# Squares of the first seven-product phase kept on chip, its loads asked for earlier, and two weight sums moved ahead

## The chip, the cores and the metric

The kernel runs on one core of one Trainium2 chip. The metric is the device time of one execution in microseconds (us). TensorE does the matrix products (PE in the rows; PEld is its weight load), VectorE (DVE) and ScalarE (ACT) move results out of PSUM and do the elementwise work, GpSimd (POOL) scales operands in SBUF, and SyncE (SP) issues nearly all DMAs from one in-order queue.

## The reference, cut to what matters

```
# attention with decay, in blocks of 64 tokens (B=4, H=8, S=768, D=64)
intra = ((q_b @ k_b.T) * Dmask) @ v_b
inter = (q_b * lam_pow) @ kv_state
out_b = intra + inter
kv_state = lam_block * kv_state + (k_b * rev_pow).T @ v_b
# feed-forward on x = attention output, 3072 tokens x 512
h = x @ w_in          # 512 -> 2048
g = relu(h) ** 2
y = g @ w_out         # 2048 -> 512
```

## The kernel before

The 3072 tokens are 24 tiles of 128, or six groups of four tiles (512 tokens). Every float32 operand of the feed-forward part is split into a high and a low part (`wh` and `wl` hold those of weights and tokens), and a product is made of three matmuls: high by high, low by high, high by low.

Groups 0 and 1 are done plainly, 16 steps `f` each: `hidden` (12 matmuls, one 128-column piece of h), `square`, then `project` of the step before (12 matmuls into four `acc` banks). I call the 16 steps of group 1 "steps 0 to 15". In even steps `go(t, t + 1)` does the attention of tile t and begins that of the tile after it; in between the weights of the later phases are prepared: `weigh(n)` forms sums of w_in and writes them to DRAM (`ws`), and `fold(n)` forms sums of w_out (VectorE: `fold_whole` and `fold_sums`; then a ScalarE cast `fold_hi` and a VectorE subtraction `fold_lo`, which issues two DMAs to DRAM, `wt`). The dictionary `todo` says in which step a cast and its subtraction stand.

Groups 2 and 3 are then done together, as a 2 by 2 block product with seven products in place of eight. This is the first seven-product phase: eight blocks `quad(n)`, n = 0 to 7, each with `product(n, 0)` to `product(n, 6)` of six matmuls each, and between products 2 and 3 the attention `go(t)` of tile t = 16 + n. The weights of a product come from DRAM through the tile `ring`, asked for eight products ahead, by `stream(k + 8)` at the end of each product. A block gives four 128-column results: two sums `gs`, which live in four tiles `GT` and are squared in place one block later (`square_pair`), and two (`pa` and `pb`, in PSUM) that `square_in` squares into `E[2n]` and `E[2n + 1]`. The order of the work on each engine is the order in which the code stands.

Before the change, `E[0]` to `E[11]` are slices of `GT[2]` and `GT[3]`. These are needed for `gs` from block 4 on, so squares 0 to 7 are copied to DRAM (`es`, blocks 0 to 3) and read back in block 7 (`move` with a source), and squares 8 to 11 are copied on chip into free columns of `w_out` (`spare`). The loads of k, q, v of tile t + 2 (`load_qk`, `load_kv`) stand at the end of a block, behind `state`, and GpSimd's scaling of k (`scale_k`) behind them. `fold(0)` to `fold(5)` are done in blocks 1 to 6, and `fold(7)`, `fold(6)` in steps 0 and 1.

Then `gather_all(2)` multiplies by w_out, again with seven products, in 16 passes q of about 5 us: eight for one half of the result (squares `E`) and eight for the other (`GT`). Pass q reads the sums of one `fold`, which `fold_in` asks for two passes ahead, and the operands that `operands`, `operands_hi`, `operands_lo` prepare three passes ahead. `SEQ` is the order of the folds in the first eight passes: 4, 5, 6, 0, 7, 1, 2, 3. `between(q)` stands behind pass q: it reads the attention outputs (`ks`, eight DMAs) into `GT[0]` and `GT[1]`, forms their sums, and `rows_of` writes the operands of the second seven-product phase (`quad_all`, groups 4 and 5).

In `go`, ScalarE reads one element of the first attention bank into `mark`; TensorE's next writes to that bank wait for this read.

```
        product(n, 2, pd, True, False)
        go(t, None if last else t + 1, True)
        product(n, 3, pb, False, False)
        add(gs[1], pb, p1)
        product(n, 4, pa, False, True)
        square_in(f, pa)
        product(n, 5, pb, False, True)
        product(n, 6, pd, False, True)
        add(pb, pb, p1)
        add(gs[0], pd, gs[0])
        square_in(f + 1, pb)
```

Of the kernel before, what the change touches and what calls it, by code (L numbers as in the profile page):

```python
# [7 lines left out]
F32 = mybir.dt.float32  # L8
# [27 lines left out]
def body(ctx: ExitStack, tc: tile.TileContext, qT, kT, kvq, lam, w, out):  # L36
# [60 lines left out]
    def w_out(f):  # L97
        return NF + (f + 1) % NF
# [316 lines left out]

    def masked_by_half(t):
        a = wk.tile([P, 2, NPR, D], F32, name="a")
# [18 lines left out]

    def go(t, after, own=False):
        po, pn = (ps_acc, "acc") if own else (ps_a, "att")
        qo, qn = (ps_acc, "acc") if own else (ps_h, "h")
        o = [po.tile([P, DM], F32, name=pn) for _ in range(2)]  # L440
# [135 lines left out]
    def f32(x):  # L576
        return x.bitcast(F32)
# [141 lines left out]
    def fold_lo(n):  # L719
        x, (hi, lo) = FOLD.pop(n)  # L720
        sub(lo, x.rearrange("p a b -> p (a b)"), f32(hi))
        for i, y in enumerate((hi, lo)):
            nc.sync.dma_start(out=wt[n, :, :, i], in_=f32(y).rearrange("p (a b) -> p a b", a=4))

    E, OPS, TR = {}, {}, [None, None]
    GT = []
    es = dram.tile([NF // 2, P, DM], F32, name="es")
    ks = dram.tile([2 * G, P, DM], F32, name="ks")
    squares, spill = [], []

# [3 lines left out]
    def first_places():  # L734
        for tag in ("xh", "xl"):
            GT.append(wk.tile([P, 4, N], F32, name="gs", tag=tag))
        for tag in ("xh", "xl"):
            GT.append(wk.tile([P, 4, N], F32, name="gs", tag=tag))
        for f in range(3 * NF // 4):
            E[f] = GT[3 if f > 3 else 2][:, f % 4]  # L740

    def spare(i):
        j = w_out(4 * i)
        return [f32(x[:, j : j + 3 : 2, 2 * P :]) for x in (wh, wl)]

    def move(n, x, source=None):
        for j in range(2):
            f = 2 * n + j
            nc.sync.dma_start(out=x[j], in_=by_half(E[f] if source is None else source[f]))
            E[f] = x[j]  # L750

# [4 lines left out]
    def square_pair(n):  # L756
        x = GT[n // 2][:, 2 * n % 4 : 2 * n % 4 + 2].rearrange("p a b -> p (a b)")
        nc.scalar.activation(x, x, AF.Relu)
        nc.scalar.activation(x, x, AF.Square)

    def quad(n, prev):
        f, t = 2 * n, 4 * G + n
        last = n == NF // 2 - 1
        if n == 0:
            first_places()
        gs = [GT[n // 2][:, f % 4 + j] for j in range(2)]
        pa, pb = (ps_h.tile([P, N], F32, name="h") for _ in range(2))
        pd = ps_a.tile([P, N], F32, name="att")
        p1 = wk.tile([P, N], F32, name="p1", tag="gh")
        KEPT[t] = wk.tile([P, DM], F32, name="kept", tag="gl")  # L770
        product(n, 0, pa, True, False)
        nc.scalar.copy(p1, pa)
        if n:
            square_pair(n - 1)
        product(n, 1, pb, True, False)
        add(gs[0], pb, p1)
        if n > 1:
            fold_lo(n - 2)
        if n in (5, 6):
            move(n - 1, spare(3 * (6 - n)))  # L780
        if last:
            move(0, spare(1), es)
            move(1, spare(2), es)
            x = io.tile([P, 2 * DM], F32, name="qk_sb")
            move(2, [by_half(x[:, j * DM : (j + 1) * DM]) for j in range(2)], es)
            operands(1)
        if n == 0:
            project(*prev)
        product(n, 2, pd, True, False)
        if last:  # L790
            open_folds(0)
        go(t, None if last else t + 1, True)
        if not last:
            scale_q(t + 1)
        product(n, 3, pb, False, False)
# [8 lines left out]
        if n == NF // 2 - 2:  # L804
            for j in range(2):
                E[f + j] = mask.rearrange("p j a c -> p j (a c)")[:, j]
        if last:
            for j in range(2):
                E[f + j] = wk.tile([P, N], F32, name="kept", tag="a")
        square_in(f, pa)  # L810
        if 0 < n < NF // 2 - 1:
            fold(n - 1)
        product(n, 5, pb, False, True)
        if last:
            operands_hi(2)
        product(n, 6, pd, False, True)
        if last:
            open_folds(1)
            add(gs[0], pd, gs[0])
            operands_lo(1)  # L820
            operands(3)
            operands_hi(3)
            add(pb, pb, p1)
        else:
            add(pb, pb, p1)
            add(gs[0], pd, gs[0])
        square_in(f + 1, pb)
        if last:
# [4 lines left out]
        else:  # L833
            if n:
                fold_hi(n - 1)
            state(t, False)
            state(t + 1, True)
            if t + 2 < NT:
                load_qk(t + 2)
                load_kv(t + 2)  # L840
                scale_k(t + 2)
        nc.sync.dma_start(out=ks[n], in_=kept(t))
        if n < NF // 4:
            for j in range(2):
                nc.sync.dma_start(out=es[f + j], in_=E[f + j])
        if last:
            move(3, [by_half(x.rearrange("p a c -> p (a c)")) for x in (qpow, kv)], es)
        if n == NF // 2 - 2:
            operands(0)
# [25 lines left out]

    def quad_all(n):
        f = 2 * n
# [12 lines left out]
        add(u2, pb, p1)  # L890
        places_for(f)
        if last:
            operands(1)
# [36 lines left out]

    NQ = NF // 2
    SEQ = [4, 5, 6, 0, 7, 1, 2, 3] + list(range(NQ))
    MAP = [2, 0, 3, 1]
# [6 lines left out]
    def fold_in(q, j):  # L940
        if q < 2 * NQ:
            nc.sync.dma_start(
                out=f32(TR[q % 2][:, j]), in_=wt[SEQ[q], :, (1, 0, 2, 3)[j]].rearrange("p a b -> p (a b)")
            )

    def operands(q):
        par, n = q // NQ, SEQ[q]
# [37 lines left out]
    def gather(q, i, bank):  # L985
        k, n = q % NQ, SEQ[q]
        f = 2 * n
# [77 lines left out]
    def between(q):  # L1065
        two = [slice(0, 2), slice(2, 4)]
        flat = [[x[:, h].rearrange("p a d -> p (a d)") for h in two] for x in GT]
        (e0, e1), (d0, d1), (n0, n1), (f0, f1) = flat
        if q in (6, 8):
            j = (q - 6) // 2  # L1070
            for i in range(G):
                nc.sync.dma_start(
                    out=GT[j][:, :, i * C : (i + 1) * C], in_=ks[2 * i + j].rearrange("p (a b) -> p a b", a=KT)
                )
        if q == 10:
            sub(n0, d0, e0)
            sub(n1, d1, n0)
        if q == 12:
            sub(f0, d1, d0)
            sub(f1, e1, e0)  # L1080
            sub(f1, f1, f0)
            rows_of(8, GT[2][:, two[1]])
        if q == 13:
            rows_of(0, GT[0][:, two[0]])
# [195 lines left out]
    for f in range(NF):  # L1280
# [23 lines left out]
        if f % 2 == 0:  # L1304
# [5 lines left out]
            load_kv(t + 2)  # L1310
        if f < 2:
            fold(NF // 2 - 1 - f)
        if f in WEIGH:
# [16 lines left out]
    gather_all(2, between)  # L1330
    SEQ[:NQ] = range(NQ)
    MAP[:] = [3, 0, 2, 1]
    ORDER[:] = [0, 4, 6, 5, 1, 3, 2]
    for n in range(NF // 2):
        quad_all(n)
    gather_all(4, lambda q: None)
# [54 lines left out]
```

## Time and profile before

| | |
|---|---|
| time, median of 3 runs | 628.91 us (627.04, 628.91, 637.31) |
| the profiled execution: time / span | 625.99 us / 624.3 us |
| PE busy, DVE busy, ACT busy (share of the span) | 93%, 71%, 48% |
| chain that ended last: PE, DMA, DVE, issue | 55%, 14%, 13%, 7% |
| bytes moved by DMA | 145.58 MB, mean 233 GB/s |

A time in a row is counted from the start of the span. In brackets behind an instruction stands how long its engine had been idle and what ended that. "Clock" is the TensorE clock that the chip granted; 1.00 is 2.4 GHz, 0.5 is 1.2 GHz.

### The profile page before, as it was taken

Reading aid. Unit: us, or ns where it says so; the run is one execution under the profiler, and the core shown is the slowest. Engines: PE = TensorE matmul, PEld = TensorE weight load, DVE = VectorE, ACT = ScalarE, POOL = GpSimd, SP = SyncE. Lnnn points to the kernel's source line nnn. Section 1 sums busy time; section 2 is a strip of 40 time slices with the busy share of each in tenths; the row PEclk is TensorE's granted clock in tenths of the full one; section 3 lists DMA queues with packets and bytes.
Section 4 is the critical chain, followed back from the end, with each engine's and each line's share of the span. In section 5 each row is a group of like instructions: output and inputs, shape, how many; then the busy total and the mean of one; then the engine's idle time right before and its main releaser. Section 6 shows DMA issues by size and latency. Waiting matters only on the chain.

```text
span 624.3 us, 13452 instructions
## 1 busy us (share of the span) xinstructions
PE 580.3 (93%) x5308; PEld 501.4 (80%) x5308; DVE 442.2 (71%) x734; ACT 297.5 (48%) x522; POOL 96.0 (15%) x106
## 2 busy tenths in 40 slices
PE   9998999998999998788888879998969999999997
PEld 7886888887887886666666669997958888899997
DVE  6899999748887767355555699579564455997942
ACT  4678787544455553444444484343223233652420
POOL 5321213314322223102122100000000000000000
PEclk9999999999999999999979989999989999999999
DMA  8847656235998874769879887698666777676863
GB/s 307 334 141 250 220 201 207 97 135 180 305 362 295 279 234 139 246 204 307 287 248 321 264 307 240 212 303 273 186 203 183 221 194 201 205 227 205 278 205 122
DMA packets 88909, 145.58 MB, mean 233 GB/s; under 512 B 7952, under 2 KB 40720, under 8 KB 88848
## 3 DMA queue, kind: packets, MB, share of 16 engines
q1 hardware_dynamic: 84208, 139.49, 69.4%
q10 hardware_dynamic: 4640, 5.24, 2.3%
q8 instruction: 42, 0.69, 0.5%
q14 instruction: 19, 0.16, 0.1%
HBM read 109.05 MB, written 33.55 MB: 228 GB/s over the span
## 4 chain that ended last, share of the span: by engine, by line
PE 55%; DMA 14%; DVE 13%; issue 7%; SPq 3%; ACT 3%; POOL 2%; ACTq 0%; DVEq 0%; POOLq 0%
PE h L674 13%; PE acc L998 13%; PE h L514 6%; PE att L998 6%; DMA kv_sb<-in_kvq 6%; PE att L674 4%; PE h L998 3%; DMA folds<-wt 3%; DVE sums L214 2%; DMA ws<-parts 2%; PE acc L544 2%; PE acc L549 2%; PE acc L545 2%; DVE rec L214 2%; POOL kv_sb L395 1%
## 5 line engine op out<-in xcount | busy, mean ns | idle before, releaser
L674 PE MATMUL h<-wh,ring 128*128 128x512 f32 x320 | 92.1, 411 | 8.6 <-DVE kv_sb L214 5.3
L674 PEld LDWEIGHTS h<-wh,ring 128*128 128x128 f32 x320 | 62.0, 198 | 24.9 <-DVE kv_sb L214 6.1
L998 PE MATMUL acc<-folds,wh 128*128 128x256 f32 x384 | 71.6, 286 | 6.7 <-DMA folds<-wt 6.7
L998 PEld LDWEIGHTS acc<-folds,wh 128*128 128x128 f32 x384 | 60.7, 194 | 7.0 <-issue 7.0
L970 ACT CAST wh<-sums 128x1024 fp32r<-128x1024 f32 x32 | 33.6, 1050 | 52.8 <-DVE sums L214 16.7
L998 PE MATMUL acc<-folds,wl 128*128 128x256 f32 x192 | 54.9, 286 | 0.0
L214 DVE TENSOR_TENSOR wl<-sums,wh 128x1024 fp32r<-128x1024 f32 x38 | 46.3, 1219 | 8.3 <-ACT wh L970 8.3
L674 PE MATMUL h<-wl,ring 128*128 128x512 f32 x160 | 51.7, 405 | 0.0
L544 PE MATMUL acc<-wh,gh 128*128 128x512 f32 x128 | 50.3, 393 | 0.0
L549 PE MATMUL acc<-wh,gl 128*128 128x512 f32 x128 | 49.9, 390 | 0.0
L545 PE MATMUL acc<-wl,gh 128*128 128x512 f32 x128 | 49.9, 390 | 0.0
L503 POOL TENSOR_TENSOR kvd<-kv,qpow 128x256 f32<-128x256 f32 x27 | 21.8, 807 | 123.0 <-DVE kv L214 101.3
L521 ACT ACTIVATE h<-h 128x512 f32<-128x512 f32 x32 | 18.7, 584 | 45.0 <-PE h L514 44.8
L529 DVE TENSOR_TENSOR gl<-h,gh 128x512 fp32r<-128x512 f32 x32 | 21.9, 684 | 23.6 <-ACT h L524 23.6
L998 PEld LDWEIGHTS acc<-folds,wl 128*128 128x128 f32 x192 | 37.4, 195 | 0.0
L674 PEld LDWEIGHTS h<-wl,ring 128*128 128x128 f32 x160 | 31.5, 197 | 7.3 <-issue 0.3
L214 DVE TENSOR_TENSOR gs<-h,p 128x512 f32<-128x512 f32 x16 | 11.1, 691 | 36.4 <-PE h L674 35.8
L514 PE MATMUL h<-xh,wh 128*128 128x512 f32 x128 | 36.0, 403 | 0.8 <-DVE a L214 0.2
L514 PE MATMUL h<-xh,wl 128*128 128x512 f32 x128 | 34.5, 391 | 1.6 <-DVE wl L159 1.6
L674 PE MATMUL att<-wh,ring 128*128 128x512 f32 x128 | 34.4, 390 | 0.0
L514 PE MATMUL h<-xl,wh 128*128 128x512 f32 x128 | 34.3, 389 | 0.0
L214 DVE TENSOR_TENSOR wl<-gs,wh 128x256 fp32r<-128x256 f32 (+2 forms) x39 | 25.8, 672 | 11.2 <-ACT wh L1062 9.6
(252 smaller groups left out, 1425.0 us busy)
## 6 DMA issues: line engine op xcount, KB each, us to landing
folds<-wt SPq DMA_DIRECT2D x128, 256.0 KB, 3.9
ring<-ws SPq DMA_DIRECT2D x112, 256.0 KB, 3.1
raw<-in_w SPq DMA_DIRECT2D x30, 512.0 KB, 4.3
kv_sb<-in_kvq SPq DMA_DIRECT2D x22, 512.0 KB, 5.8
ws<-parts SPq DMA_DIRECT2D x32, 256.0 KB, 4.4
qk_sb<-in_kT SPq DMA_DIRECT2D x22, 256.0 KB, 4.3
qk_sb<-in_qT SPq DMA_DIRECT2D x22, 256.0 KB, 4.7
out_x<-qk_sb ACTq DMA_DIRECT2D x16, 256.0 KB, 6.4
```

What stands on the lines that cost most here:

```text
L214: lambda o, x, y, op=op: V.tensor_tensor(out=o, in0=x, in1=y, op=op)
L395: nc.gpsimd.tensor_tensor(out=x, in0=x, in1=y.broadcast_to([P, NPR, 2, D]), op=ALU.mult)
L503: nc.gpsimd.tensor_tensor(out=kvd, in0=d, in1=qpow[:, :, D - 1 : D].broadcast_to([P, NPR, D]), op=ALU.mult)
L514: nc.tensor.matmul(h, wt[:, f, kt * P : (kt + 1) * P], x[:, kt], start=k == 0, stop=k == 11)
L521: nc.scalar.activation(h, h, AF.Relu)
L529: V.tensor_tensor(out=gl, in0=r, in1=gh.bitcast(F32), op=ALU.subtract)
L544: nc.tensor.matmul(accs[m][i], gh[:, cs], wh[:, j], start=f == 0, stop=False)
L545: nc.tensor.matmul(accs[m][i], gh[:, cs], wl[:, j], start=False, stop=False)
L549: nc.tensor.matmul(accs[m][i], gl[:, cs], wh[:, j], start=False, stop=end)
L674: nc.tensor.matmul(bank, x[:, part_, kt], t[:, q + kt], start=start and z == 0, stop=stop and z == 5, skip_group_check=True,)
L970: nc.scalar.copy(o_, x)
L998: nc.tensor.matmul(bank[:, r * 2 * P : (r + 1) * 2 * P], x, y, start=k == 0 and r == 0 and z == 0, stop=k == NQ - 1 and z == 2, skip_group ...
```

## The change

- Loads: `load_qk(t + 2)` and `load_kv(t + 2)` stand directly behind `go(t)` in the middle of the block. `scale_k(t + 2)` stays at the end.
- Squares: the DRAM tile `es` is gone (8 DMAs out, 8 back, of 256 KB each). `E` gets 16 homes on chip; nine squares are copied on chip at the ends of blocks 1, 2, 4, 5, 6 (`MOVES`). In return `p1`, `kept` and the attention tile `a` have one buffer each in the phase, not two.
- Sums of w_out: `fold(7)` before step 0, `fold(6)`, `fold(5)`, `fold(4)` in steps 0, 1, 8; `fold(0)` to `fold(3)` in blocks 1 to 4, spread over two blocks each.
- Order: `add(pb, pb, p1)`, the second `square_in` and both `state` stand ahead of product 6; in block 0 `project` stands ahead of products 0 and 1.
- Passes: the folds are read in their natural order; the DMAs of `between` stand behind passes 9 and 11 (were 6 and 8), its sums and `rows_of` one or two passes later, and `rows_of(6)`, `rows_of(4)` stand in the first block of `quad_all` (`late`).

```diff
-    def go(t, after, own=False):
+    def go(t, after, own=None):
...
-            masked_by_half(after)
+            masked_by_half(after, own)
...
+        only.extend(wk.tile([P, N], F32, name=n, tag=t) for n, t in (("p1", "gh"), ("kept", "gl"), ("a", "a")))
+        more = [wk.tile([P, N], F32, name="kept", tag=t) for t in ("gh", "gl")]
+        homes = [t2[:, i] for i in range(4)] + more + [None, t3[:, 0], t3[:, 1], t3[:, 2], t3[:, 0], t3[:, 3]]
+        homes += [m_[:, 0], m_[:, 1], only[2], qpow.rearrange("p a c -> p (a c)")]
...
+    MOVES = {1: ((0, 6), (1, 7)), 2: ((2, 4), (3, 5)), 4: ((7, 0),), 5: ((8, 1), (9, 2), (10, 3))}
...
         if n == 0:
+            project(*prev)
             first_places()
...
-        p1 = wk.tile([P, N], F32, name="p1", tag="gh")
-        KEPT[t] = wk.tile([P, DM], F32, name="kept", tag="gl")
+        p1, KEPT[t], a_at = only
...
-        if n > 1:
-            fold_lo(n - 2)
-        if n in (5, 6):
-            move(n - 1, spare(3 * (6 - n)))
...
-        go(t, None if last else t + 1, True)
+        if 0 < n < NQ - 3:
+            fold_whole(n - 1)
+        go(t, None if last else t + 1, a_at)
+        if t + 2 < NT:
+            load_qk(t + 2)
+            load_kv(t + 2)
...
+        if 1 < n < NQ - 2:
+            fold_hi(n - 2)
+            fold_lo(n - 2)
...
-        if 0 < n < NF // 2 - 1:
-            fold(n - 1)
         product(n, 5, pb, False, True)
         if last:
             operands_hi(2)
+        else:
+            add(pb, pb, p1)
+            square_in(f + 1, pb)
+            state(t, False)
+            state(t + 1, True)
         product(n, 6, pd, False, True)
...
+        if 0 < n < NQ - 3:
+            fold_sums(n - 1)
+        if t + 2 < NT:
+            scale_k(t + 2)
         nc.sync.dma_start(out=ks[n], in_=kept(t))
-        if n < NF // 4:
-            for j in range(2):
-                nc.sync.dma_start(out=es[f + j], in_=E[f + j])
+        for e, i in MOVES.get(n, ()):
+            move(e, spare(i))
+        if n == NQ - 2:
+            move(11, by_half(io.tile([P, 2 * DM], F32, name="qk_sb")[:, 0:DM]))
             operands(0)
...
-        if q in (6, 8):
-            j = (q - 6) // 2
+        if q in (9, 11):
+            j = (q - 9) // 2
...
-            rows_of(6, GT[3][:, two[1]])
-            rows_of(4, GT[1][:, two[1]])
+
+    def late():
+        rows_of(6, GT[3][:, 2:4])
+        rows_of(4, GT[1][:, 2:4])
...
+    FOLDS = {0: 6, 1: 5, 8: 4}
...
+    fold(NF // 2 - 1)
```

## Rows read from the trace of the kernel before

**Rows 1.** Stretches (us; busy us of each engine, granted clock, DMA share, GB/s): blocks 4, 5.

```profile
303.00:322.00 19.00, 15.60 (x172) 12.17 (x171) 9.15 (x18) 7.92 (x16) 3.52 (x4) 0.82 0.78 251
322.00:336.80 14.80, 12.36 (x172) 10.10 (x171) 7.88 (x15) 7.14 (x15) 3.54 (x4) 1.00 0.97 316
```

**Rows 2.** Waits of PE, 232 to 372 us: total, times, longest.

```profile
PE acc L426 <- POOL kv_sb L395: 8.6, 6, 2.8
PE acc L411 <- DMA qk_sb<-in_qT: 5.2, 5, 1.4
PE acc L998 <- DMA folds<-wt: 3.6, 1, 3.6
PE h L674 <- ACT gs L754: 2.0, 4, 0.6
```

**Rows 3.** Timeline of PE: starts of blocks 1 and 7, attention of block 2.

```profile
254.96 1.07 PE L674 MATMUL h<-wh,ring 128*128 128x512 f32 x4
...
276.83 0.45 PE L446 MATMUL acc<-qk_sb,kv 64*64 64x64 f32 x8
278.78 0.69 PE L411 MATMUL acc<-qk_sb 64*64 64x64 f32 x32 [1.50 <-issue]
...
281.18 0.68 PE L426 MATMUL acc<-kv_sb 64*64 64x64 f32 x28 [0.89 <-POOL kv_sb L395]
281.79 1.19 PE L674 MATMUL h<-wh,ring 128*128 128x512 f32 x4
...
352.82 1.07 PE L674 MATMUL h<-wh,ring 128*128 128x512 f32 x4
```

**Rows 4.** Chain that ended last: start, length, what; passes 0, 1, later products.

```profile
369.59 3.52 PE acc L998 x18
...
375.62 2.88 PE acc L998 x24
...
472.26 2.72 PE h L674 x12
```

**Rows 5.** DMA issues, 237 to 365 us: count, KB each, median us to landing.

```profile
kv_sb<-in_kvq SPq DMA_DIRECT2D x6, 512.0 KB, 6.4
...
ks<-kept SPq DMA_DIRECT2D x7, 256.0 KB, 6.5
...
wh<-gs SPq DMA_DIRECT2D x2, 256.0 KB, 8.0
```

**Rows 6.** Timeline of SP: the second `ks` reads of `between`.

```profile
421.58 2.54 SPq L1072 DMA_DIRECT2D gs<-ks  x4
```

**Rows 7.** Timeline of PE: steps 2 and 10, pass 11, first block of `quad_all`.

```profile
148.95 0.69 PE L411 MATMUL h<-qk_sb 64*64 64x64 f32 x30 [1.71 <-DVE gl L529]
...
202.99 0.74 PE L411 MATMUL h<-qk_sb 64*64 64x64 f32 x32
...
429.76 0.48 PE L998 MATMUL acc<-folds,wh 128*128 128x256 f32 x2 [3.02 <-DMA folds<-wt]
...
464.02 2.07 PE L674 MATMUL h<-wh,ring 128*128 128x512 f32 x4 [5.26 <-DVE kv_sb L214]
```

**Rows 8.** Timeline of ACT: step 0, first block of `quad_all`.

```profile
132.52 1.08 ACT L557 COPY o<-acc 128x512 f32<-128x512 f32 x2
134.04 0.15 ACT L462 COPY mark<-att 1x1 f32<-1x1 f32 x1 [0.44 <-PE att L446]
...
458.80 2.94 ACT L1062 CAST wh<-gs 128x1024 fp32r<-128x1024 f32 x3 [6.97 <-issue]
```

**Rows 9.** Timeline of DVE: steps 1 and 10, first block of `quad_all`.

```profile
139.41 0.43 DVE L214 TENSOR_TENSOR sums<-rec 128x256 f32<-128x256 f32 x1 [1.71 <-DMA out_x<-o]
...
202.31 0.68 DVE L529 TENSOR_TENSOR gl<-h,gh 128x512 fp32r<-128x512 f32 x1
203.50 1.23 DVE L214 TENSOR_TENSOR parts<-sums,parts 128x1024 fp32r<-128x1024 f32 x1 [0.51 <-ACT parts L596]
...
459.88 3.50 DVE L214 TENSOR_TENSOR wl<-gs,wh 128x1024 fp32r<-128x1024 f32 x3 [2.23 <-ACT wh L1062]
```

More of the change, by code (lines that the diff above doesn't have):

```diff
@@ L414, in scores_by_half, with masked_by_half @@
                     )
-    def masked_by_half(t):
-        a = wk.tile([P, 2, NPR, D], F32, name="a")
+    def masked_by_half(t, at=None):
+        a = wk.tile([P, 2, NPR, D], F32, name="a") if at is None else at.rearrange("p (j a d) -> p j a d", j=2, a=NPR)
         for j, x in enumerate(sc_of.pop(t)):
@@ L435, in open_half @@
         part_of[t] = sc_of[t][1]
-    def go(t, after, own=False):
-        po, pn = (ps_acc, "acc") if own else (ps_a, "att")
-        qo, qn = (ps_acc, "acc") if own else (ps_h, "h")
+    def go(t, after, own=None):
+        po, pn = (ps_acc, "acc") if own is not None else (ps_a, "att")
+        qo, qn = (ps_acc, "acc") if own is not None else (ps_h, "h")
         o = [po.tile([P, DM], F32, name=pn) for _ in range(2)]
@@ L723, in fold_lo @@
             nc.sync.dma_start(out=wt[n, :, :, i], in_=f32(y).rearrange("p (a b) -> p a b", a=4))
+    NQ = NF // 2
     E, OPS, TR = {}, {}, [None, None]
     GT = []
-    es = dram.tile([NF // 2, P, DM], F32, name="es")
     ks = dram.tile([2 * G, P, DM], F32, name="ks")
-    squares, spill = [], []
     def by_half(x):
@@ L738, in first_places, with move @@
             GT.append(wk.tile([P, 4, N], F32, name="gs", tag=tag))
-        for f in range(3 * NF // 4):
-            E[f] = GT[3 if f > 3 else 2][:, f % 4]
-    def spare(i):
-        j = w_out(4 * i)
-        return [f32(x[:, j : j + 3 : 2, 2 * P :]) for x in (wh, wl)]
-    def move(n, x, source=None):
-        for j in range(2):
-            f = 2 * n + j
-            nc.sync.dma_start(out=x[j], in_=by_half(E[f] if source is None else source[f]))
-            E[f] = x[j]
+        (t2, t3), m_ = GT[2:], mask.rearrange("p j a c -> p j (a c)")
+        only.extend(wk.tile([P, N], F32, name=n, tag=t) for n, t in (("p1", "gh"), ("kept", "gl"), ("a", "a")))
+        more = [wk.tile([P, N], F32, name="kept", tag=t) for t in ("gh", "gl")]
+        homes = [t2[:, i] for i in range(4)] + more + [None, t3[:, 0], t3[:, 1], t3[:, 2], t3[:, 0], t3[:, 3]]
+        homes += [m_[:, 0], m_[:, 1], only[2], qpow.rearrange("p a c -> p (a c)")]
+        for f in range(NF):
+            E[f] = homes[f]
+    only = []
+    def spare(i):
+        j = w_out(4 * (i // 2))
+        return f32((wh, wl)[i % 2][:, j : j + 3 : 2, 2 * P :])
+    def move(f, x):
+        nc.sync.dma_start(out=x, in_=by_half(E[f]))
+        E[f] = x
     def square_in(f, h):
@@ L791, in quad @@
             open_folds(0)
-        go(t, None if last else t + 1, True)
+        if 0 < n < NQ - 3:
[4 more added lines that the diff above has]
+            load_kv(t + 2)
         if not last:
             scale_q(t + 1)
+        if n == 3:
+            E[6] = wk.tile([P, N], F32, name="kept", tag="a")
         product(n, 3, pb, False, False)
@@ L803, in quad @@
             operands(2)
[L804 to L809, printed above, removed]
         square_in(f, pa)
-        if 0 < n < NF // 2 - 1:
-            fold(n - 1)
         product(n, 5, pb, False, True)
@@ L818, in quad @@
             open_folds(1)
-            add(gs[0], pd, gs[0])
+        add(gs[0], pd, gs[0])
+        if last:
             operands_lo(1)
@@ L823, in quad @@
             add(pb, pb, p1)
[L824 to L828, printed above, removed]
+            square_in(f + 1, pb)
             square_pair(n)
@@ L874, in places_for, with quad_all @@
             E[f + k] = y
-    def quad_all(n):
+    def quad_all(n, then):
         f = 2 * n
@@ L891, in quad_all @@
         places_for(f)
+        if then is not None:
+            then()
         if last:
@@ L942, in fold_in @@
             nc.sync.dma_start(
-                out=f32(TR[q % 2][:, j]), in_=wt[SEQ[q], :, (1, 0, 2, 3)[j]].rearrange("p a b -> p (a b)")
+                out=f32(TR[q % 2][:, j]), in_=wt[q % NQ, :, (1, 0, 2, 3)[j]].rearrange("p a b -> p (a b)")
             )
     def operands(q):
-        par, n = q // NQ, SEQ[q]
+        par, n = q // NQ, q % NQ
         f = 2 * n
@@ L985, in gather @@
     def gather(q, i, bank):
-        k, n = q % NQ, SEQ[q]
+        k, n = q % NQ, q % NQ
         f = 2 * n
@@ L1074, in between @@
                 )
-        if q == 10:
+        if q == 12:
             sub(n0, d0, e0)
             sub(n1, d1, n0)
-        if q == 12:
+        if q == 13:
+            rows_of(8, GT[2][:, two[1]])
             sub(f0, d1, d0)
@@ L1310, in body @@
             load_kv(t + 2)
-        if f < 2:
-            fold(NF // 2 - 1 - f)
+        if f in FOLDS:
+            fold(FOLDS[f])
         if f in WEIGH:
@@ L1334, in body @@
     for n in range(NF // 2):
-        quad_all(n)
+        quad_all(n, late if n == 0 else None)
     gather_all(4, lambda q: None)
```

28 lines of the change are left out of this document (2 added, 26 removed).

## The prediction

> **What bounds the kernel now.** I first read the stretches of the first seven-product phase [rows 1]: no engine is full. TensorE is busy for 15.6 of 19.0 us in block 4 and for 12.4 of 14.8 in block 5, and the DMA engines are at a share of 0.78 and 0.97. So TensorE waits there, and the view of its waits says for what [rows 2]: 8.6 us for GpSimd's scaling of k (`scale_k`, which itself follows the load), 5.2 us for the loads of k and q, 2.0 us for ScalarE's squares, and, behind the phase, 3.6 us for the first sums of w_out. The timeline shows the pattern in one block [rows 3]: attention of block 2 runs from 276.83 to 281.79 with two pauses, 1.50 (called "issue", but at the place where other blocks wait for q) and 0.89 us.
>
> What would a block take without pauses? A product of six matmuls takes 1.36 us (12 take 2.72 [rows 4]), seven take 9.5; attention without its pauses 4.96 - 1.50 - 0.89 = 2.6. With restarts 12.2 us. Blocks 1 to 6 take 352.82 - 254.96 = 97.9 us [rows 3], the floor is 6 x 12.2 = 73.2. The gap of 24.7 us holds the waits (8.6 + 5.2 + 1.5 + 2.0 = 17.3) and 7.4 us of restarts and of reduced clock: in block 4 the granted clock was 0.82 on average, so part of it was at 1.2 GHz, behind a pause of 2.8 us [rows 1, 2].
>
> **The change, part by part.** Times within a block are from its start: product 3 begins at 6.7, product 6 ends at 12.2.
>
> *Loads.* They now stand behind attention. The buffer of tile t + 2 is that of tile t, so SP can issue k and q when attention has read q (about 5.6) and k, v of the token layout at its end (6.8), in place of 12.5 and later. With the landing of 6.4 us [rows 5] they are there at 13.2; the next attention wants them at 12.2 + 5.9 = 18.1. The slack of 4.9 us covers GpSimd's scaling, which stands behind the same two fades as before. Past whom do the loads move? On SP past the ring requests of products 3 to 6, which wait for those products anyway, and past the DMAs of a fold; so nothing ready is held up. The pauses for GpSimd and loads go, and the reduced clock with them.
>
> *Second square.* The sum of `pb` and its square no longer wait behind product 6; `pb` is free before product 1 of the next block wants it. The 2.0 us go. `state` ahead of product 6 and `gs[0]` behind it shift VectorE's work by about one product; the next reader of `gs[0]` (`square_pair`) stands a product later. The mask multiplication must now wait for the old `a` to be read (one buffer); VectorE is idle there, at 0.
>
> *What takes the place of the waits.* Three buffers are tighter. First, `E[10]` lies in the slice that block 6 overwrites with its first sum `gs[0]`, due at 2.9. Its on-chip copy is third behind the `ks` write at the end of block 5, so issued at about 14.2. Such copies landed 8.0 us after issue [rows 5]: 22.2, or 10.0 in block 6. Product 3 accumulates into the bank that this sum reads, so it would start at 10.7 in place of 6.7: 4.0 us; with a landing under 4.7 us nothing. The row was taken under the same load (a fold's DMAs ahead), so I stay near it: 3 us. Second, `kept` has one buffer: `ks` is asked for at 12.6, lands at 19.1 (6.5 us [rows 5]), 6.9 in the next block, where ScalarE wants to write at 6.8. Some 0.7 us more are covered, since cast, subtraction and squares still end before `pb` is wanted; each further microsecond is paid in full: 0 to 1 us in each of four blocks. Third, `E[7]`'s copy (13.1 + 8.0 = 8.9 in block 5) is due at 9.6. For the last two and for loads that queue behind more copies I take 2 us. Blocks 1 to 6: -24.7 + 3 + 2 = **-19.7** (bounds -24.7 and -12).
>
> *Block 0.* `project` first, so that its banks are copied out before attention wants them; its low part waits some 0.3 us for VectorE. VectorE's two copies then end about a microsecond earlier. **-1.0** (0 to -1.5).
>
> *First folds.* In block 7 the requests for the first folds stood behind a fold's write and six copies from `es`; these are gone, and the folds 0 and 1 were written long before. The request goes out when product 2 frees the buffer, 7 us ahead of need. The wait of 3.6 us goes [rows 2], and the slow start behind it: 18 matmuls took 3.52 us where 24 take 2.88, so 18 take 2.16 [rows 4], 1.4 us. **-5.0** (-3.6 at least).
>
> *`between`.* The second set of `ks` reads stood in SP's queue at 421.58 until pass 10's and 11's operands had left `GT[1]` [rows 6]; the folds of pass 11 were behind it, and TensorE waited 3.02 us [rows 7]. Behind pass 11 the tile has long been read. The sums come later and VectorE's work for the last passes is packed tighter, but `rows_of` there waits for TensorE as before. **-3.0** (-2 at least, if the reads now hold the folds of passes 13 and 14 a little).
>
> *`rows_of`.* At the start of `quad_all` TensorE waited 5.26 us for the sum that frees `pb` [rows 7]; ahead of it stood three casts (2.94 us [rows 8]) and three subtractions (3.50 us [rows 9]). Two of each leave. The sum then follows one subtraction (to 461.1) and comes at about 461.1 in place of 463.3: **-2.2**. The two rows that are left to `late` are wanted by products 5 and 6, 2.7 us later, and cost 0 to 0.5. The reduced clock behind the stall I leave as it is.
>
> *Price in steps 0 to 9.* `fold(7)` moved up is free by itself (VectorE is idle ahead of step 0's sums). But its cast now stands ahead of the copies out of the `acc` banks [rows 8], and the third of these waits for the subtraction of 1.23 us [rows 9], since both share the buffers tagged `A`. `mark` comes at about 135.5 in place of 134.04, and TensorE's attention with it: 1.5 us. The output DMAs follow later and behind 1 MB of sums, so the sums of the next fold, which waited for them until 139.41 [rows 9], wait until about 141. From there to step 2's pause (until 148.95, for VectorE's `gl` [rows 7]) VectorE is full: that end moves by 1.6 us, which includes the 1.5. `fold(4)`: its sums fit into VectorE's idle time of step 9, its subtraction (1.23 us) does not: it stands ahead of `gl` of step 10, which ended at 202.99 just as TensorE began [rows 7, 9]. 1.2 us. **+2.8** (1.5 to 5, if VectorE also collides with GpSimd).
>
> *Sum.* -19.7 - 1.0 - 5.0 - 3.0 - 2.2 + 2.8 = **-28.1 us**. From the profiled execution of 626.0 us: 597.9. The median of the runs shown is 2.9 us above that execution, so **601 us** against 628.9. About 2% is what a measurement of this kernel can tell from no change: 616 us and below is faster.
>
> **A rate as a bound.** Packed tighter, blocks 2 to 5 carry 18.35 MB: each 1.84 of ring, 1.05 of loads, 0.26 of `ks`, 1.05 of a fold, and six copies of 0.26 in all. In block 5 of before, 316 GB/s came at a share of 0.97 [rows 1], so 326 at a full share: 56.3 us for four blocks whose floor is 48.8, 7.5 more. That is a rival below; against it speaks that part of that share is queueing that the waits themselves caused. The Trainium skill ("DMA: Bandwidth & Descriptors", section "Bandwidth") gives about 358 GB/s as the memory's share for one core: an estimate from it is 51.3 us, 2.5 more than the floor in place of 7.5. No row of a whole block here reaches that rate.
>
> **The rivals.**
> 1. *The DMA engines become the bound.* At 326 GB/s blocks 2 to 5 cost 7.5 us more than the floor; the hand-backs of 5 us are then mostly inside it, say 2 remain beside: 601 + 7.5 + 2 - 5 = 606, and up to 609 where the waits come at reduced clock again. For it: the share of 0.97. Against: eight reads and eight writes of `es` and two folds leave the phase.
> 2. *The loads don't get earlier in effect.* If copies and folds queue ahead and they land only 11 us after issue, GpSimd's and the loads' pauses stay. Then the blocks give back only the 2.0 of the squares and some clock, about 4: 626.0 - 4 - 1 - 5 - 3 - 2.2 + 2.8 + 2.9 = 616.5. Against: no median landing in the rows is over 8.0.
> 3. *Slower: the single `kept` closes a ring.* ScalarE's copies at 6.8, `ks` at 12.6, landing L, next copies: a block lasts 5.8 + L when L is long. Before, a block lasted 97.9 / 6 = 16.3. The other parts give 8.4 us, or 1.4 a block, so from L = 11.9 us on the kernel is slower than before, and at L = 14 it is 642. Against: L was 6.5 [rows 5] and fewer DMAs stand ahead.
>
> **How the numbers follow.** Forecast (601): 0.68. Rival 1 (606 to 609): 0.17. Rival 2 (616): 0.10. Rival 3 (over 629): 0.05. The low end: no hand-back (-5), steps 0 to 9 at 1.5 (-1.3), and the median as near to the profile as it can be (-2.9): 592. The high end takes in rival 1 with 2 us more in steps 0 to 9: 611. Range 592 to 611. Rival 2 stands on the border and is counted with "within 2%": faster 0.85, within 2% 0.11, slower 0.04.
>
> **What the profile after would show.** Blocks 1 to 5 of 12.2 to 13 us each; TensorE's waits on GpSimd's scaling, k and q nearly gone there, with a clock of 1.00; a pause of 0 to 4 us ahead of product 3 in block 6, put down to VectorE or a copy; no wait for folds at the first pass and none in pass 11; a stall of about 3 us, not 5.3, at the first block of `quad_all`; steps 2 and 10 later by 1.6 and another 1.2 us. Blocks of 14 us and more with a DMA share near 1 would be rival 1; ScalarE's copies to `kept` waiting for the `ks` write would be rival 3. The prediction is most wrong if those landings grow, since three of its buffers live on them.

## The result and the profile after

The changed kernel takes **597.7 us** (median of 4 runs, 596.7 to 598.9) against 628.9 us of the kernel before (three runs that were made with it, 627.0 to 631.1); the ratio is 0.950 (95% interval 0.946 to 0.955). A fourth run of the kernel before, 637.3 us, was in a slower state of the chip and is left out. The prediction was 601 us, 592 to 611. The profiled execution took 598.24 us, its span is 596.5.

Stretches of the whole kernel say where the time came from. The columns are: from and to, length, busy us (instructions) of TensorE, its weight loads, VectorE, ScalarE and GpSimd, granted clock, DMA share, GB/s. The seven lines are: up to step 0, steps 0 to 15, block 0, blocks 1 to 6, block 7, the 16 passes, the rest from `quad_all` on. (`project` stood inside block 0 before and stands ahead of it now; lines 2 and 3 are cut at the hidden products of step 15, so that they compare.) First the kernel before:

```profile
0.00:127.84 127.84, 123.74 (x976) 101.19 (x977) 111.74 (x154) 87.41 (x123) 38.94 (x51) 1.00 0.62 215
127.84:231.67 103.83, 101.28 (x1355) 83.53 (x1352) 77.61 (x131) 53.06 (x119) 31.44 (x28) 1.00 0.80 265
231.67:254.96 23.29, 21.25 (x207) 17.21 (x207) 15.28 (x28) 10.50 (x27) 5.64 (x5) 1.00 0.47 148
254.96:352.82 97.86, 79.79 (x990) 63.21 (x988) 49.08 (x93) 43.90 (x89) 19.40 (x22) 0.95 0.86 280
352.82:365.08 12.26, 11.40 (x108) 8.84 (x106) 10.68 (x22) 10.19 (x20) 0.62 (x1) 1.00 0.70 213
365.08:454.31 89.23, 82.56 (x674) 82.21 (x672) 68.85 (x120) 35.17 (x54) 0.00 (x0) 0.98 0.78 251
454.31:624.30 169.99, 160.27 (x1010) 145.22 (x1008) 108.98 (x191) 57.23 (x93) 0.00 (x0) 0.98 0.68 205
```

The same seven of the kernel after:

```profile
0.00:127.41 127.41, 124.48 (x976) 101.86 (x976) 111.45 (x154) 87.39 (x123) 39.66 (x51) 1.00 0.63 215
127.41:237.66 110.25, 104.07 (x1357) 85.80 (x1353) 85.58 (x145) 54.93 (x121) 33.07 (x28) 0.97 0.80 268
237.66:260.77 23.11, 21.37 (x206) 17.07 (x207) 15.58 (x29) 10.62 (x27) 5.70 (x6) 1.00 0.50 162
260.77:337.38 76.61, 72.99 (x990) 59.69 (x988) 47.58 (x81) 44.06 (x89) 20.46 (x23) 0.98 0.94 327
337.38:348.75 11.37, 11.10 (x107) 8.92 (x106) 8.31 (x18) 8.92 (x19) 0.55 (x1) 1.00 0.51 162
348.75:429.38 80.63, 80.63 (x673) 80.63 (x672) 68.02 (x120) 35.01 (x54) 0.00 (x0) 1.00 0.79 252
429.38:596.50 167.12, 159.19 (x1010) 144.44 (x1008) 109.38 (x191) 57.22 (x93) 0.00 (x0) 0.98 0.69 208
```

The differences are -0.4, **+6.4**, -0.2, **-21.3**, -0.9, **-8.6** and **-2.9**: -27.8 us, the whole difference of the spans. Length less busy time is TensorE's idle time: in blocks 1 to 6 it was 18.1 us and is 3.6, so 14.5 of the 21.3 us are pauses that went. The other 6.8 are busy time (79.8 to 73.0) for the same 990 matmuls. The granted clock accounts for about half of that: at 0.95 over 97.86 us some 4.9 us were lost, at 0.98 over 76.61 us some 1.5 are. The rest is busy time at full clock, as far as the rows tell largely in attention, which the pauses had cut up: its matmuls took 2.6 us in block 2 before (4.96 less the two pauses [rows 3]) and take about 2.3 in a block without pauses. In the passes TensorE now has no idle time at all.

The blocks by themselves, in the kernel after (same columns; blocks 2, 3, 5 and 6, each counted from its product 1 to product 1 of the next; they answer to [rows 1]):

```profile
274.00:285.80 11.80, 11.80 (x156) 9.75 (x155) 8.55 (x16) 7.75 (x15) 2.46 (x4) 1.00 1.00 331
285.80:298.10 12.30, 12.00 (x171) 9.50 (x169) 8.72 (x16) 7.65 (x16) 3.74 (x4) 1.00 1.04 370
...
310.10:322.00 11.90, 11.90 (x172) 9.82 (x171) 8.16 (x15) 7.64 (x15) 3.75 (x5) 1.00 1.05 385
322.00:338.70 16.70, 13.43 (x171) 10.90 (x170) 4.97 (x10) 6.69 (x14) 3.50 (x4) 0.90 0.70 230
```

Blocks 2 and 5 are full of TensorE's work from end to end at a clock of 1.00; only block 6 has a pause. It stands in TensorE's timeline after, with the larger pauses that are left elsewhere (start, length, instruction; in brackets the idle time ahead and what ended it):

```profile
151.56 1.02 PE L411 MATMUL h<-qk_sb 64*64 64x64 f32 x27 [3.42 <-DVE gl L529]
...
154.76 2.07 PE L514 MATMUL h<-xh,wh 128*128 128x512 f32 x4
...
209.01 0.69 PE L411 MATMUL h<-qk_sb 64*64 64x64 f32 x30 [0.91 <-DVE gl L529]
...
330.18 1.33 PE L674 MATMUL h<-wh,ring 128*128 128x512 f32 x4 [3.27 <-DVE gs L214]
...
437.45 2.07 PE L674 MATMUL h<-wh,ring 128*128 128x512 f32 x4 [3.23 <-DVE kv_sb L214]
```

The first, second and last of these bracketed rows answer to [rows 7]: step 2 (1.71 us before), step 10 (none before) and the first block of `quad_all` (5.26 before). The third is new and was forecast: product 3 of block 6. Four matmuls take 1.07 us at the full clock; 2.07 behind a pause is 1.2 GHz. VectorE's timeline says who made TensorE wait:

```profile
140.79 1.29 DVE L214 TENSOR_TENSOR rec<-wh,wl 128x512 f32<-128x512 f32 x2 [4.55 <-ACT gh L523]
142.04 0.42 DVE L214 TENSOR_TENSOR sums<-rec 128x256 f32<-128x256 f32 x1
...
329.43 0.69 DVE L214 TENSOR_TENSOR gs<-h,p 128x512 f32<-128x512 f32 x1 [6.94 <-DMA wl<-gs]
```

At 329.43 the sum `gs[0]` of block 6 had been waiting for a copy `wl<-gs`: `E[10]` leaving the slice. The sums of step 1's fold start at 142.04, where they started at 139.41 before [rows 9]. (The first row names ScalarE's `gh`, which ended at the same time; what `rec` needs is buffers that the output DMAs read, and in the trace the second of these DMAs lands at 140.67.) And the landings in the seven-product phase (246 to 348 us), which answer to [rows 5]:

```profile
kv_sb<-in_kvq SPq DMA_DIRECT2D x6, 512.0 KB, 5.7
...
ks<-kept SPq DMA_DIRECT2D x7, 256.0 KB, 4.9
...
wh<-gs SPq DMA_DIRECT2D x4, 256.0 KB, 5.2
wl<-gs SPq DMA_DIRECT2D x4, 256.0 KB, 4.9
...
ring<-ws SPq DMA_DIRECT2D x48, 256.0 KB, 5.0
```

The first four are shorter than before (6.4, 6.5, 8.0 and 7.8), although more bytes a microsecond move. The last, the weights of the products, got longer; before (237 to 365 us) it was

```profile
ring<-ws SPq DMA_DIRECT2D x48, 256.0 KB, 4.0
```

### The profile page after: what moved, and what is told of

Same layout as the page of the kernel before. It is cut to its first block, busy times and chain, and to the rows that moved or that the text cites. A ratio compares the mean times of both kernels' runs of the same rounds, so it can differ in the third digit from the quotient of the medians.

```text
span 596.5 us, 13421 instructions
## 1 busy us (share of the span) xinstructions
PE 573.8 (96%) x5308; PEld 498.4 (84%) x5308; DVE 445.9 (75%) x734; ACT 298.2 (50%) x522; POOL 99.4 (17%) x106
## 4 chain that ended last, share of the span: by engine, by line
PE 69%; DVE 11%; issue 7%; DMA 6%; ACT 3%; POOL 2%; SPq 1%; ACTq 0%; DVEq 0%; POOLq 0%
PE h L674 17%; PE acc L991 15%; PE att L991 7%; PE h L514 6%; PE att L674 6%; PE h L991 4%; DMA ws<-parts 3%; PE acc L544 2%; PE acc L549 2%; PE acc L545 2%; DVE parts L214 2%; DMA ws<-wh 1%; DVE sums L214 1%; PE acc L446 1%; DVE rec L214 1%
## 5 line engine op out<-in xcount | busy, mean ns | idle before, releaser
L674 PE MATMUL h<-wh,ring 128*128 128x512 f32 x320 | 89.2, 401 | 6.9 <-DVE gs L214 3.3
L674 PEld LDWEIGHTS h<-wh,ring 128*128 128x128 f32 x320 | 60.5, 192 | 21.2 <-DVE kv_sb L214 4.1
L214 DVE TENSOR_TENSOR wl<-sums,wh 128x1024 fp32r<-128x1024 f32 x36 | 43.9, 1219 | 6.4 <-ACT wh L963 4.3
L514 PEld LDWEIGHTS h<-xh,wl 128*128 128x128 f32 x128 | 24.2, 190 | 7.3 <-DVE wl L159 2.0
L549 PEld LDWEIGHTS acc<-wh,gl 128*128 128x128 f32 x128 | 24.0, 188 | 5.9 <-DVE gl L529 0.8
```

Source lines behind the costliest of these rows:

```text
L214: lambda o, x, y, op=op: V.tensor_tensor(out=o, in0=x, in1=y, op=op)
L514: nc.tensor.matmul(h, wt[:, f, kt * P : (kt + 1) * P], x[:, kt], start=k == 0, stop=k == 11)
L549: nc.tensor.matmul(accs[m][i], gl[:, cs], wh[:, j], start=False, stop=end)
L674: nc.tensor.matmul(bank, x[:, part_, kt], t[:, q + kt], start=start and z == 0, stop=stop and z == 5, skip_group_check=True,)
```

## The experiments

Eleven kernels; each median stands beside runs of the kernel before on the same chip. The ratio of the change itself, 0.950 (0.946 to 0.955), is what they are held against.

**e1, the loads put back alone.**

```
-        (load_qk, load_kv of t + 2 behind go)
+        (load_qk, load_kv of t + 2 ahead of scale_k, at the block's end)
```

> The changed kernel with one edit undone: the loads of k, q, v of tile t + 2 stand at the end of the block again, ahead of scale_k. Theory (the place of the loads made the gain): TensorE's waits on GpSimd's scaling and on k and q come back in blocks 1 to 6, 8.6 + 5.2 + 1.5 us of before, with restarts and reduced clock, so blocks 1 to 6 last 14 to 20 us more than the 76.6 us of the changed kernel, and the time is 612 to 618. Rival (the relief of the DMA engines made it: no es traffic, two folds fewer): the loads now land fast from their old place too, blocks 1 to 6 last at most 6 us more, 604 or less.

Measured: 624.0 us, ratio 0.992 (0.989 to 0.995). The direction is the theory's, the size is larger: 26 us in place of 14 to 20, most of the 31 gained. Blocks 1 to 6 took 106.9 us, more than before:

```profile
259.72:366.64 106.92, 88.80 (x989) 72.46 (x988) 43.72 (x81) 44.36 (x89) 19.39 (x23) 0.82 0.73 237
```

TensorE's waits in the phase (238 to 375 us; total, times, longest):

```profile
PE acc L411 <- DMA qk_sb<-in_qT: 14.1, 6, 3.2
PE acc L426 <- POOL kv_sb L395: 2.8, 5, 1.0
```

Idle time is 18.1 us, as before the change; busy time is 88.8, which is 9.0 more than before and 15.8 more than after, at a granted clock of 0.82 in place of 0.95 and 0.98. So the loads carry two prices: the pauses themselves, and the reduced clock behind them.

**e2, the loads moved alone, in the kernel before.** The same edit the other way round.

```
         go(t, None if last else t + 1, True)
+        if t + 2 < NT:
+            load_qk(t + 2)
+            load_kv(t + 2)
```

> The kernel before with one edit alone: the loads of k, q, v of tile t + 2 stand directly behind the attention. Squares still go through es, the folds stand where they stood. Theory (place of the loads): of the 24.7 us above the floor in blocks 1 to 6 the waits on loads and GpSimd (15.3), and most of the 7.4 us of restarts and reduced clock go, the waits for squares (2.6) stay: 15 to 20 us less than before, 610 to 615. Rival (the DMA engines were the bound, share 0.92 to 0.97 in these blocks): blocks stay above 14 us, at most 6 us less than before.

Measured: 609.6 us, ratio 0.968 (0.960 to 0.976), as the theory had it. Stretch of blocks 1 to 6, and TensorE's waits from 232 to 372 us (total, times, longest):

```profile
254.85:335.09 80.24, 74.18 (x990) 59.44 (x988) 49.72 (x94) 43.90 (x89) 19.48 (x22) 0.98 0.96 329
```

```profile
PE acc L999 <- DMA folds<-wt: 3.9, 1, 3.9
...
PE h L674 <- ACT gs L754: 2.8, 5, 0.6
```

The phase falls from 97.9 to 80.2 us by this alone, with the writes and copies of `es` still there. The folds' wait and the squares' wait stay. The whole change brings the phase to 76.6 us, only 3.6 less, and 2.8 us of e2 are the squares' waits; so, as far as this comparison goes, the traffic of `es` itself cost little in these blocks. No run takes `es` out alone.

**e3, no copy for `E[10]` to wait for.** The ninth and tenth results change homes and the copies go a block earlier.

```
-    MOVES = {..., 4: ((7, 0),), 5: ((8, 1), (9, 2), (10, 3))}
+    MOVES = {..., 3: ((7, 0),), 4: ((8, 1), (9, 2)), 5: ((10, 3),)}
```

> The changed kernel with other homes for squares 9 and 10 and earlier copies: E[9] in the slice of E[7], E[10] in the slice that E[9] had; E[7] is copied at the end of block 3, E[8] and E[9] at the end of block 4, E[10] at the end of block 5. Nothing that block 6 overwrites first is copied late then. Theory: the pause of 3.27 us ahead of product 3 in block 6 goes, and the reduced clock behind it (products 3 and 4 took 1.98 and 2.47 us there, 1.50 and 1.38 in block 5): 3.3 + 1.6 = 4.9 us less than the changed kernel, 593. Rival (the pause is not of that copy but of DMAs that queue at the end of block 5 in general): the pause stays over 2 us or moves to blocks 4 and 5, within 1.5 us of the changed kernel.

Measured: 593.0 us, ratio 0.941 (0.935 to 0.946). Product 3 of block 6 follows attention without a pause and at full clock (four matmuls in 1.21 us, 1.33 with the pause of 3.27 ahead):

```profile
326.50 1.21 PE L674 MATMUL h<-wh,ring 128*128 128x512 f32 x4
327.55 0.62 PE L674 MATMUL h<-wl,ring 128*128 128x512 f32 x2
```

**e4, no fold ahead of step 0.**

```
-    FOLDS = {0: 6, 1: 5, 8: 4}            (and fold 7 ahead of step 0)
+    FOLDS = {0: 7, 1: 6, 8: 5, 12: 4}
```

> The changed kernel with the four early sums of w_out in steps 0, 1, 8 and 12 (folds 7, 6, 5, 4), none ahead of step 0. Theory: the price of steps 0 to 9 (6.4 us: mark 1.1 late, step 2's pause 3.42 in place of 1.71, 6.8 us at 1.2 GHz behind it, 0.9 in step 10) comes from the cast and subtraction of fold 7 in step 0, which hold back the copies out of the acc banks and the output DMAs whose buffers the next fold wants. Then step 2's pause is 1.7 again at full clock, 0.9 stays in step 9 or 10 and up to 1.2 comes in steps 13 and 14: 593 to 595. Rival (VectorE's 9 us of two more folds cost the same wherever they stand): 597 to 599.

Measured: 595.5 us, ratio 0.944 (0.937 to 0.951), between the two; the interval overlaps that of the change, and the steps of the trace carry the reading. Steps 0 to 15 took 4.1 us less (106.2, from 110.3). The pause of step 2 is what it was before the change, and no reduced clock follows:

```profile
148.99 0.69 PE L411 MATMUL h<-qk_sb 64*64 64x64 f32 x30 [1.61 <-DVE gl L529]
```

Some of that came back at block 6, where this profile shows a pause of 3.9 us and a longer stretch at 1.2 GHz. The size of that pause differs between profiles of kernels with nothing changed there (2.6 to 5.3 us over e4, e5, e6, e7 and e9), which blurs comparisons of a few microseconds.

**e5, the second square put back behind product 6.**

```
         product(n, 6, pd, False, True)
+        add(pb, pb, p1)
         add(gs[0], pd, gs[0])
+        square_in(f + 1, pb), then the two steps of state
```

> The changed kernel, with the sum of pb, its square and the two state steps back behind product 6 in blocks 0 to 6. Theory (the prediction's term for the second square): the wait of TensorE for ScalarE's squares, 0.4 to 0.6 us a block in the kernel before, 2.0 in all, comes back ahead of product 1 of the next block, with perhaps as much again from gs[0] coming earlier or later: 600 to 602 us, and a row of TensorE waiting for ScalarE's gs behind pb in five or six blocks. Rival: now that the loads are early, VectorE and ScalarE have room and the square ends in time anyway: 597 to 599 us and no such row.

Measured: 596.7 us, ratio 0.950 (0.944 to 0.957): the rival. ScalarE squares `pb` right behind VectorE's sum, and TensorE waits for neither:

```profile
281.95 0.58 ACT L757 ACTIVATE h<-h 128x512 f32<-128x512 f32 x1 [0.88 <-DVE h L214]
```

**e9, the folds' parts put back in VectorE's and ScalarE's order.** Since e5 cleared the square's place, the next suspect was the fold's sums in front of the sum of `pb`.

```
+        square_in(f, pa)
+        if 0 < n < NQ - 3:
+            fold(n - 1)
         product(n, 5, pb, False, True)
```

> The changed kernel with the parts of the folds of blocks 1 to 4 back at the places that they had before in the orders of VectorE and ScalarE (sums between product 4 and product 5, cast behind the second square, subtraction and write behind product 1 of the next block). Nothing else moves; the square stands where the change put it. Theory: what held the second square, and TensorE's product 1 of the next block behind it, was the fold's sums in front of the sum of pb on VectorE; with them back the wait of 0.4 to 0.6 us returns in blocks 1 to 4, 2 to 3 us in all: 599.5 to 601 us, with a row of TensorE waiting for ScalarE's gs four or five times. Rival: the folds' place is as free as the square's: 597 to 599 us.

Measured: 597.8 us, ratio 0.948 (0.944 to 0.953). The trace shows the theory's mechanism, the time does not show it. ScalarE's square waits for VectorE 2.13 us instead of 0.9 (first row, end of block 2), and TensorE for the square (second row, product 1 of block 3), four times, once in each of blocks 2 to 5; from product 3 to product 3 these blocks' periods are 12.67, 12.69, 12.86 and 12.69 us, where they are 11.79, 11.84, 12.53 and 11.84 after.

```profile
283.97 0.58 ACT L757 ACTIVATE h<-h 128x512 f32<-128x512 f32 x1 [2.13 <-DVE h L214]
285.23 1.20 PE L674 MATMUL h<-wh,ring 128*128 128x512 f32 x4 [0.56 <-ACT kept L758]
```

That is 2.9 us, and the profiled span is still 2.0 shorter than after: block 0 took 1.5 less (a pause marked "issue" is missing), block 6 0.7 less, the rest behind the phase 2.0 less. So the cause of the squares' wait is shown (the places of the fold's parts together); that its removal is worth 2 us in the median is not.

**e6, the `ks` reads back at passes 6 and 8.**

```
-        if q in (9, 11):
+        if q in (6, 8):
```

> The changed kernel, with the two sets of ks reads back at passes 6 and 8 of the gather (the sums stay where the change put them). Theory (the prediction's term): the second set stands in SP's queue until the operands of passes 10 and 11 have left GT[1], the folds of pass 11 queue behind it and TensorE pauses for about 3 us in pass 11, with reduced clock behind it: 600.5 to 602.5 us. Rival: the 3 us were due to the place of the sums on VectorE, not to the reads: no pause for folds, 597 to 599 us.

Measured: 601.2 us, ratio 0.958 (0.951 to 0.964), as the theory had it. The pause is back in pass 11, as in [rows 7]:

```profile
413.01 0.50 PE L991 MATMUL acc<-folds,wh 128*128 128x256 f32 x2 [4.08 <-DMA folds<-wt]
```

**e7, the remaining `rows_of` out of the way of the first sum.** Two go behind the sum that frees `pb`, one behind the next.

```
         product(n, 1, pb, True, False)
         add(u2, pb, p1)
+        rows_of(2, ...), rows_of(6, ...)
...
         add(u3, pb, p1)
+        rows_of(4, ...)
```

> The changed kernel, with all three remaining rows_of of the second slice taken from in front of the first block of the last phase: two behind the sum that frees pb, one behind the next sum. Theory: the stall of 3.23 us at 437.45 is VectorE's and ScalarE's row work in front of that sum; it falls to 1 to 2 us, and the half clock behind it (3.4 us) may go too: 595 to 596.5 us. Rival: the sum is held by the copies that come before it, and the rows only come late where products 5 and 6 want them: the stall stays at 2.5 to 3.2 us or moves to product 5 or 6, 597.5 to 600 us.

Measured: 595.9 us, ratio 0.947 (0.942 to 0.953): the theory's size, though the intervals overlap. The stall is 1.11 us instead of 3.23, and the part from `quad_all` on takes 165.2 us instead of 167.1:

```profile
432.47 1.20 PE L674 MATMUL att<-wh,ring 128*128 128x512 f32 x4 [0.89 <-DVE qk_sb L214]
435.24 1.20 PE L674 MATMUL h<-wh,ring 128*128 128x512 f32 x4 [1.11 <-DVE kv_sb L214]
```

**e8, twelve more writes of 256 KB in blocks 0 to 5.**

```
+        if n < 6:
+            for j in range(2):
+                nc.sync.dma_start(out=es[f + j], in_=E[f + j])
         for e, i in MOVES.get(n, ()):
```

> The changed kernel with twelve more writes of 256 KB (3.1 MB in all) that nobody reads: E[f] and E[f + 1] to memory at the end of each of blocks 0 to 5, where the kernel before had its writes to es. The output stays the reference's. Theory: the DMA engines have room in these blocks (385 GB/s came in one of 11.9 us), so the blocks stay at 11.8 to 12.6 us and the time at 597.5 to 600 us. Rival (the prediction's rival 1, a rate as the bound): each block must carry 0.52 MB more, 1.4 to 1.6 us at 326 to 385 GB/s, in blocks 1 to 5 some 8 us: 604 to 607 us, with TensorE waiting for ring, k and q there.

Measured: 603.8 us, ratio 0.961 (0.956 to 0.966). That is the low end of the rival's range, but reached another way. Stretches of blocks 3, 4 and 5 (counted here from product 3 of the block before, so with its second half; the last two end 0.7 and 1.3 us ahead of the next product 3):

```profile
277.50:289.30 11.80, 11.80 (x176) 9.80 (x171) 9.47 (x17) 7.74 (x15) 3.61 (x5) 1.00 0.95 303
289.30:303.00 13.70, 11.68 (x135) 8.98 (x134) 8.45 (x16) 7.63 (x15) 3.56 (x5) 1.00 1.05 393
303.00:316.00 13.00, 11.84 (x150) 9.09 (x141) 9.80 (x16) 7.63 (x15) 3.65 (x4) 1.00 1.04 384
```

Up to 289 us the writes cost nothing (11.8 us a block). Then the DMA engines stand at a share of 1.05 and 393 GB/s, and from product 3 to product 3 the next two blocks take 14.44 and 13.55 us, where they take 12.53 and 11.84 after; but TensorE never waits for ring, k or q. It waits for squares behind a late `kept` (ScalarE's copy waits 4.93 us for the `ks` write), and at block 6 for the copy of `E[10]`, issued at 330.18 in place of 324.43:

```profile
336.62 0.69 DVE L214 TENSOR_TENSOR gs<-h,p 128x512 f32<-128x512 f32 x1 [11.21 <-DMA wl<-gs]
```

TensorE's pause there is 7.64 us in place of 3.27: 4.4 of the 8.0 us between the two spans (this execution, 606.3 us, is the slowest of the four). The theory, that the engines have room, holds for the first blocks and falls for the phase. The changed kernel, at 385 GB/s in block 5, is close to the highest rate of these rows (393), and what gives way first in e8 are the hand-backs (buffers that are free again only when a transfer out of them has landed), not the loads.

**e10, e1 with the folds' writes out of the loads' way.** I took the excess of e1 for loads that queue behind 1 MB of fold writes issued just ahead of them.

```
         product(n, 1, pb, True, False)
         add(gs[0], pb, p1)
+        (fold_hi(n - 2), fold_lo(n - 2) for blocks 2 to 5)
```

> The changed kernel with the loads of q, k, v back at the end of the block (that alone gave 624 us), and the cast, subtraction and write of a fold moved from behind product 4 to behind product 1 of the same block. Theory: with the loads back alone they queued behind 1 MB of fold writes that are issued just ahead of them; with the writes half a block earlier they land about 2 us sooner in the four blocks that have folds, and these pauses shrink: 612 to 618 us. Rival: it is the loads' own late issue that costs all of the 26 us: 621 to 627 us.

Measured: 622.4 us, ratio 0.988 (0.982 to 0.993): the rival; that theory fell. TensorE's waits in the phase only change name. In e1 they were 14.1 us for q and 2.8 for GpSimd's scaling of k, at a clock of 0.82 over blocks 1 to 6; here the clock is 0.85, and:

```profile
PE acc L426 <- POOL kv_sb L395: 9.3, 5, 2.5
PE acc L411 <- DMA qk_sb<-in_qT: 7.0, 5, 2.3
```

**e11, e3, e4 and e7 together.**

> The changed kernel with three edits together: the other homes for two of the results (no copy for E[10] to wait for), the folds of steps 0 to 12 each later (none ahead of step 0), and the remaining rows_of out of the way of the first sum of the last phase. If the gains are separate stalls they add up: 4.7 and 4 and 1.9 us from the traces of the three, 587 to 588 us. Rival: the places interact (folds later in the steps push writes against the start of the seven-product phase, copies run closer), and no more than the best single one comes: 591 to 593 us.

Measured: **587.4 us** (6 runs, 586.2 to 588.2), ratio 0.932 (0.929 to 0.935), faster than both kernels. The gains add up. The two largest waits of TensorE that are left (total, times, longest):

```profile
PE h L411 <- DVE gl L529: 3.3, 3, 1.5
PE h L514 <- DVE wl L159: 1.5, 1, 1.5
```

## Why the prediction was right

**The size.** The sum was -28.1 us from one profiled execution to the next; -27.8 was measured. The 3.3 us between 601 and 597.7 are the step from the profile to the median: I carried over the 2.9 us by which the median of before lay above its profile, and after lies 0.5 below. Inside the sum, errors cancel: the steps cost 3.6 us more than forecast, the other lines together give 3.4 more. That the total is met within 0.3 us is luck.

| term | forecast | measured |
|---|---|---|
| blocks 1 to 6 | -19.7 | -21.3 |
| block 0 | -1.0 | -0.2 |
| block 7 | 0 | -0.9 |
| first folds and `between` (passes) | -8.0 | -8.6 |
| `rows_of` (from `quad_all` on) | -2.2 | -2.9 |
| steps 0 to 15 | +2.8 | +6.4 |
| up to step 0 | 0 | -0.4 |

**Loads.** Shown from both sides: e2 gives 20 us of the 31 by them alone, e1 loses 26 without them. The floor of 12.2 us was a little high: a block without pauses takes 11.8, of which the seven products are 9.5, so attention takes 2.3, not the 2.6 that I had left over from a disturbed one. Against that floor the six blocks still lose 5.8 us (76.6 less 70.8), the hand-backs and their clock, for which 5 were forecast. That the reduced clock goes with the pauses was said; its weight was not: of the 21.3 us, up to 3.4 are clock (4.9 less 1.5), and e1's excess of busy time over the kernel before (9.0 us) goes with a clock of 0.82 in place of 0.95, at the same 18.1 us of pauses. What e1 does not settle is why the clock is lower there than before at the same idle time; moving the folds' writes away hardly changes it (0.85 in e10).

**Second square.** The wait went, and its cause was named wrongly. Moving it ahead of product 6 does nothing (e5): in either place VectorE takes up the sum as soon as product 5 ends. What held it were the fold's sums (e9), which the change also moves.

**The hand-backs.** `E[10]` came as forecast: `gs[0]` of block 6 free 8.8 us into the block (10.0 forecast), pause 3.27 us (3), and e3 takes it away. The copy landed in about 5 us, not 8.0, but SP issued it at 324.4, 3.8 us into block 6 and 1.8 later than I had it, so two errors met, by luck. `kept` also bites as forecast, with ScalarE waiting up to 3.0 us for the `ks` write, and is covered: TensorE loses 0.4 us. `E[7]` costs nothing.

**First folds and `between`.** No wait is left in the passes. e6 shows that the reads' place in SP's queue is enough to bring the pause of pass 11 back, with nothing else changed. The first folds' term is seen in the traces only: the wait is there before (3.6 us) and in e2 (3.9), gone after; no run undoes this part alone.

**Block 0.** 0.2 of the forecast 1.0 us came. TensorE's wait for ScalarE's copy out of the banks (0.7 us) is gone, as described, but a pause marked "issue" grew from 0.89 to 1.33 us; the rest stays open.

**`rows_of`.** -2.2 forecast, -2.9 measured: the stall fell by 2.0 us, and 1.1 are busy time (160.3 to 159.2), with a shorter stretch at 1.2 GHz behind it. e7 shows that the rest of the stall was rows as well.

**Steps 0 to 9: the term that was off.** "2.8 (1.5 to 5)" against 6.4. The mechanism is as described (e4 takes away 4.1 of the 6.4 us), with three sizes wrong. `mark` costs TensorE 1.1 us (1.5 forecast) and `gl` of step 10 0.9 (1.2). But I let only the four sums of the next fold wait, until 141; the two additions ahead of them (`rec`) wait too, for the landing of the outputs, until 140.79, so that the sums start at 142.04, 2.6 us later than before instead of 1.6. And the pause in step 2 grew to 3.42 us, behind which the clock fell:

```profile
151.50:158.30 6.80, 6.74 (x121) 5.95 (x122) 4.88 (x10) 2.12 (x8) 1.26 (x2) 0.59 0.72 246
```

At 0.59 over 6.8 us some 2.8 us are lost (6.8 x 0.41), which is the rise of busy time in the steps (101.3 to 104.1). The price of a reduced clock behind a new pause was in none of the bounds.

**The rivals.** 1 (DMA as the bound) fell for this kernel: block 5 runs at 385 GB/s without a pause, beyond the 326 that I took for a full share; a DMA share of 0.97 was no ceiling, for the rows above read 1.05. The Trainium skill ("DMA: Bandwidth & Descriptors", section "Bandwidth") gives two figures, about 358 GB/s as a core's share when both cores of a memory domain stream, and 425 measured on a core alone. The estimate in the prediction took the first, though this program runs on one core; block 5 goes past it (385, still 363 without its one on-chip copy of 256 KB) and stays below the second. But e8 shows that there is little room left. 2 (loads no earlier in effect) fell: no wait for k or q is left. 3 (`kept` closes a ring) fell on its own condition: `ks` landed in 4.9 us, far from 11.9.

## What to carry to other kernels

When an engine waits for a load, look first for how early the load could be asked for, and price its pauses twice: once as idle time, once as the reduced clock behind them; and price every new pause in the same way. Before blaming an instruction's place, look at what the engine in front of it (here VectorE) has to do first. When buffers are tightened so that transfers hand them back, price what happens when more bytes move: in e8 the hand-backs failed first. Other homes for two results, with copies one block earlier (e3), were worth more than either of the other small edits (4.7 us, against 2.2 in e4 and 1.8 in e7).

## What was unexpected in the hardware

- Several landings got shorter when the phase got faster (k, v 6.4 to 5.7 us, copies 8.0 to 5), at 327 GB/s on average in place of 280; those of `ring` got longer (4.0 to 5.0).
- The clock behind a pause: behind 1.71 us in step 2 of before the granted clock stays at 1.00, and behind 1.61 in e4 the matmuls run on at full speed; behind 3.42, 3.27 and 3.23 us after, there are stretches at 1.2 GHz. The length of the last pause alone does not order the rows: in the kernel before, four matmuls take 2.07 us at 264.92 behind a pause of 1.92 us, with one of 1.27 shortly ahead, and in e10 at 270.03 behind 1.46 us, with one of 1.64 shortly ahead.
- Pauses marked "issue" in the last part of attention of block 0 (0.89 us before, 1.33 after, 0.8 in e3, none there in e5) and one of 3.29 in e2: no run here shows their cause.
